# A new table of step numbers for the same steps in an attention and FFN kernel

## Chip, core and metric

The kernel runs on one core of one Trainium2 chip. The time is that of the device, in microseconds, of that core; three runs are given by their median. The profile is one execution, taken by the hardware's profiler.

## What is computed

```python
def phi(x):
    proj = np.einsum('bhsd,df->bhsf', x, w_phi)
    proj = proj - np.max(np.abs(proj), axis=-1, keepdims=True)
    return np.concatenate([np.exp(proj), np.exp(-proj)], axis=-1)
q_p, k_p = (phi(q), phi(k))
kv = np.einsum('bhsf,bhsd->bhfd', k_p, v)
z = np.sum(k_p, axis=2)
num = np.einsum('bhsf,bhfd->bhsd', q_p, kv)
den = np.einsum('bhsf,bhf->bhs', q_p, z)[..., None] + 1e-06
attn = num / den                       # 8 batches, 8 heads, 576 rows, 64 wide
x = attn.transpose(0, 2, 1, 3).reshape(4608, 512)
h = x @ w_in                           # 512 -> 2048
out = (h * np.cos(h)) @ w_out          # 2048 -> 512
```

All of it is float32.

## The kernel before

The work is cut into 3678 steps. A step is a short run of instructions on one engine: TensorE (PE), VectorE (DVE), ScalarE (ACT), GpSimd (POOL), or SyncE (SP), which issues the DMAs. The program builds the steps from loops, each with the steps that it depends on and the buffers that it takes and uses; then the list ORDER gives the sequence in which they are recorded, by their numbers. Each engine works off its own steps in that sequence. So ORDER sets what stands behind what in the five queues, and with that also when a buffer comes free.

There are three kinds of work.

Attention goes in 32 units of two heads (u0 to u31). In a unit, q_mm and q_end (L550, L553) project q on PE into three PSUM banks; q_copy (L561, L563) copies them out on ACT; DVE (L567, L575, L576), POOL (L581), DVE (L585) and POOL (L589) find and subtract the maximum; exp_q (L660) is four activations on ACT. k_mm and k_end (L596, L621) project k; k_max and k_neg (L634, L637) on DVE; exp_k (L654) on ACT reads the projection in its PSUM bank, eight activations to a half. kv_mm (L700, L706) is the first product on PE, kv_out (L712) its copy on ACT, and x_mm (L735, L741) the second product, from kv and exp_q. DVE divides, transposes, and SP stores the result to DRAM (L772, L776).

The weights w_in and w_out are converted in 16 pieces: SP loads raw words, ACT scales them (L410, L411), DVE works on their bits, ACT and DVE split them in a high and a low part (wi, wo), SP stores these to DRAM and loads them again later, since only three pieces of each kind have room (r.load, L511).

The FFN goes over nine chunks of 512 tokens. Chunks wait for the attention's results of their tokens, which SP loads (L820, L823, L1097; the tokens over 512 of each batch are gathered, L1102, in eight small DMAs to a tile). The first product is plain for three chunks (L955) and in seven half-size products of 256 columns for others (L907), or of 512 columns for the last two (L1182); ACT and DVE take the cosine (L962, L963, L981, L985, L988) and split the result (gh, gl); the second product is mm2 (L1004 to L1006, L1294 to L1296). Every float32r product is three matmuls, high by high, high by low and low by high.

PSUM has eight banks of 512 columns. A step that needs a bank gets the one whose last user stands earliest in ORDER:

```python
for x in (steps[i] for i in ORDER):
    for b in x.take:
        if b.ring == "bank":
            b.slot = min(range(len(banks)), key=lambda i: last(owner[i]))
```

So with another ORDER the same step writes another bank, and waits for another reader. The other buffers are rings of fixed size (x_raw 4, gh 3, eq 3 and so on). Exponentials and cosines need different tables on ACT; where one follows the other, a table load (ACT_TABLE_LOAD) stands between.

Of the kernel before, what the change touches and what calls it, by code (L numbers as in the profile page):

```python
# [25 lines left out]
def phi_attention_then_cos_ffn(ctx: ExitStack, tc: tile.TileContext, qkT, vS, w_phi, w_in, w_out, out):  # L26
# [41 lines left out]
    class Step:  # L68
# [19 lines left out]
        0, 42, 1, 3, 1265, 2, 4, 5, 7, 44, 6, 8, 9, 59, 46, 17, 64, 10, 65, 11, 18, 19, 58, 68, 83, 23, 47, 24,  # L88
        43, 12, 27, 45, 20, 48, 124, 1266, 21, 16, 60, 22, 13, 62, 61, 14, 50, 25, 1267, 63, 26, 15, 49, 86, 30,
        28, 1268, 31, 66, 1269, 99, 1270, 67, 32, 51, 71, 1271, 84, 33, 29, 1284, 72, 103, 52, 1272, 73, 53, 85,  # L90
        140, 1273, 87, 88, 104, 57, 101, 89, 1280, 1281, 142, 100, 56, 102, 125, 108, 90, 165, 55, 141, 91, 143,
        107, 54, 144, 35, 74, 105, 69, 146, 1274, 1275, 34, 147, 1276, 106, 112, 92, 109, 1277, 70, 93, 36, 113,
        37, 38, 1278, 114, 94, 126, 150, 148, 181, 1279, 128, 127, 145, 39, 95, 129, 130, 185, 98, 182, 40, 75,
        149, 183, 97, 131, 76, 1285, 96, 132, 206, 166, 187, 153, 188, 133, 77, 134, 154, 111, 78, 1286, 115,
        168, 1287, 184, 110, 186, 79, 191, 1295, 1288, 167, 135, 222, 169, 247, 41, 170, 1289, 116, 171, 189,
        155, 137, 224, 117, 226, 156, 138, 190, 172, 136, 223, 80, 227, 1290, 139, 118, 81, 225, 151, 173, 209,
        174, 194, 152, 119, 175, 228, 207, 229, 1291, 195, 232, 230, 196, 120, 208, 1292, 248, 231, 263, 1506,
        210, 176, 288, 212, 157, 211, 1296, 213, 179, 158, 121, 178, 265, 235, 122, 177, 1511, 159, 160, 180,
        264, 192, 214, 236, 82, 1512, 237, 197, 269, 193, 215, 266, 289, 267, 216, 123, 161, 238, 1505, 268,
        271, 270, 217, 1507, 249, 272, 1297, 304, 251, 162, 219, 252, 250, 218, 306, 305, 163, 198, 253, 273,  # L100
        307, 221, 254, 1509, 199, 255, 220, 1513, 329, 233, 308, 276, 310, 311, 256, 234, 277, 1510, 200, 257,
        278, 314, 309, 1514, 1508, 312, 290, 201, 330, 1298, 240, 1299, 292, 1314, 239, 1300, 1515, 345, 293,
        1516, 279, 313, 1301, 291, 1517, 368, 347, 258, 1302, 294, 317, 348, 1303, 1518, 318, 353, 259, 202,
        349, 319, 260, 1528, 1304, 296, 261, 274, 350, 203, 262, 320, 354, 241, 204, 346, 1305, 385, 1537, 1519,
        242, 275, 1306, 164, 351, 1307, 352, 1529, 295, 384, 297, 355, 243, 298, 1538, 390, 332, 386, 331, 1530,
        1308, 244, 281, 1539, 245, 280, 387, 1309, 1531, 333, 299, 407, 335, 334, 358, 205, 1293, 1540, 336,
        303, 1520, 388, 1315, 300, 282, 283, 302, 1546, 1564, 337, 1312, 301, 246, 284, 369, 1521, 1310, 338,
        316, 285, 339, 1316, 315, 1541, 1317, 392, 1318, 370, 1319, 1522, 371, 372, 321, 389, 446, 391, 1523,
        373, 1563, 374, 322, 340, 287, 393, 286, 375, 424, 344, 1524, 323, 1547, 341, 1325, 376, 343, 324, 1320,
        423, 429, 325, 342, 394, 326, 357, 397, 377, 327, 1321, 1569, 356, 425, 378, 427, 359, 409, 1532, 1542,  # L110
        1567, 428, 1322, 398, 1525, 411, 410, 412, 1543, 1526, 1566, 1533, 430, 1565, 1548, 413, 361, 447, 432,
        1534, 1283, 1570, 485, 360, 1294, 379, 1527, 362, 383, 1535, 363, 1549, 415, 380, 1573, 1536, 1550,
        1326, 414, 382, 364, 1544, 381, 1574, 1551, 463, 1571, 1545, 1552, 468, 1572, 1553, 469, 1568, 433, 395,
        416, 426, 1554, 365, 417, 396, 1327, 1575, 1328, 1559, 472, 1560, 1329, 431, 1282, 1330, 448, 1331,
        1576, 462, 1561, 450, 502, 451, 466, 1562, 449, 1586, 408, 1577, 328, 467, 418, 366, 1578, 452, 1555,
        421, 454, 1332, 1344, 400, 1557, 524, 419, 367, 1587, 464, 420, 399, 1311, 453, 422, 436, 507, 1333,
        1621, 434, 1324, 1588, 435, 1334, 488, 1595, 1335, 465, 401, 471, 455, 508, 1336, 402, 456, 1337, 511,
        403, 487, 437, 457, 1596, 501, 489, 1579, 438, 470, 404, 459, 439, 505, 458, 405, 503, 460, 490, 475,
        440, 1338, 461, 441, 563, 442, 1323, 473, 504, 1339, 491, 527, 474, 486, 1604, 506, 493, 406, 443, 1580,
        1622, 492, 476, 444, 509, 1597, 494, 478, 1581, 1558, 495, 510, 477, 496, 540, 1605, 498, 526, 542, 500,  # L120
        479, 514, 1623, 480, 499, 1342, 481, 1598, 497, 482, 1589, 1599, 483, 528, 1582, 1590, 1627, 1606, 1583,
        515, 1591, 543, 541, 1556, 1584, 530, 1607, 1592, 1585, 1625, 546, 1608, 1593, 1600, 544, 1609, 545,
        1601, 529, 1594, 1624, 1345, 1626, 445, 532, 525, 1602, 564, 531, 1610, 1629, 1603, 1346, 1631, 547,
# [1317 lines left out]
```

## Time and profile before

| | |
|---|---|
| median of 3 runs | 1037.19 us (1036.08 to 1038.19) |
| span of the profiled execution | 1034.7 us |
| mean granted TensorE clock | 0.998 |
| PE busy | 1024.1 us, 99% |
| weight loads (PEld) | 865.8 us, 84% |
| DVE, ACT, POOL busy | 742.0, 786.6, 147.6 us |
| first matmul starts, last ends | 1.12 us, 1031.0 us |

The times of the rows below are microseconds from the start of that execution. A timeline row gives the start, the time from the first start to the last end of the instructions that it merges, engine, line and operation, the tiles written and read (buffer numbers left out), shape and count; in brackets stands the idle time of the engine just before and what ended it. Float32 matmuls (L550 to L741) leave two records each, the others one. Matmuls are pipelined, and their ends are modelled.

### The profile page before, as it was taken

How to read it: one execution, taken by the hardware profiler on the slowest of the kernel's cores; microseconds unless marked ns; L12 is line 12 of the kernel's file. 1: busy time of each engine (PE TensorE's matmuls, PEld its weight loads, DVE VectorE, ACT ScalarE, POOL GpSimd, SP SyncE). 2: the span in 40 equal slices, each digit the busy share in tenths (PEclk: the TensorE clock that was granted, in tenths of full speed). 3: DMA queues.
4: the chain of work that ended last, by engine and by line, in shares of the span. 5: the costliest groups of instructions: out<-in, count | busy, mean ns of one | idle time of the engine just before them, and what ended most of it. 6: DMA issues, size and time to landing. Idle time of an engine off the chain costs nothing.

```text
span 1034.7 us, 23513 instructions
## 1 busy us (share of the span) xinstructions
PE 1024.1 (99%) x9402; PEld 865.8 (84%) x9402; DVE 742.0 (72%) x1418; ACT 786.6 (76%) x1602; POOL 147.6 (14%) x231
## 2 busy tenths in 40 slices
PE   9998999999999999999999999999999999999998
PEld 6786788888878888988889898888889988888886
DVE  7999998999888877765677457686565566655542
ACT  6999999898778778787789958887678465655432
POOL 4342242201101001201112011132001000000000
PEclk9999999999999999999999999999999999999999
DMA  7666587247667644678336762567427823453134
GB/s 252 192 213 207 177 257 248 89 159 256 222 232 273 209 137 158 224 262 304 116 112 218 254 234 69 176 239 257 162 77 249 293 74 92 166 210 153 41 133 153
DMA packets 86893, 195.22 MB, mean 189 GB/s; under 512 B 20608, under 2 KB 41216, under 8 KB 82944
## 3 DMA queue, kind: packets, MB, share of 16 engines
q1 hardware_dynamic: 86640, 193.66, 55.4%
q8 instruction: 74, 1.21, 0.5%
q14 instruction: 35, 0.29, 0.1%
q10 hardware_dynamic: 144, 0.07, 0.0%
HBM read 145.46 MB, written 48.23 MB: 187 GB/s over the span
## 4 chain that ended last, share of the span: by engine, by line
PE 89%; DVE 4%; ACT 3%; DMA 2%; issue 1%; SPq 0%; ACTq 0%; DVEq 0%
PE bank L907 15%; PE bank L955 10%; PE bank L1004 9%; PE bank L1005 9%; PE bank L1006 9%; PE bank L1182 8%; PE bank L700 6%; PE bank L735 5%; PE bank L1295 3%; PE bank L1294 3%; PE bank L1296 3%; PE bank L550 3%; PE bank L596 3%; PE bank L706 1%; PE bank L642 1%; PE bank L553 1%
## 5 line engine op out<-in xcount | busy, mean ns | idle before, releaser
L1004 PE MATMUL bank<-wo,gh 128*128 128x512 f32 x448 | 179.3, 400 | 0.0
L1005 PE MATMUL bank<-wo,gh 128*128 128x512 f32 x448 | 175.1, 391 | 0.0
L1006 PE MATMUL bank<-wo,gl 128*128 128x512 f32 x448 | 174.9, 390 | 0.0
L589 POOL TENSOR_TENSOR pq<-pq,bq 128x288 f32<-128x288 f32 x128 | 114.0, 922 | 174.2 <-DVE bq L585 123.5
L654 ACT ACTIVATE ek<-bank,mk 128x128 f32<-128x128 f32 x464 | 128.2, 418 | 4.6 <-DVE mk L637 4.4
L54 DVE TENSOR_TENSOR gl<-g,gh 128x512 fp32r<-128x512 f32 x128 | 89.4, 702 | 31.7 <-ACT gh L49 31.2
L49 ACT ACTIVATE gh<-g 128x512 fp32r<-128x512 f32 x128 | 81.3, 641 | 28.4 <-DVE g L988 13.3
L1004 PEld LDWEIGHTS bank<-wo,gh 128*128 128x128 f32 x448 | 84.3, 188 | 19.4 <-issue 2.2
L981 DVE SCALAR_TENSOR_TENSOR g<-g,hs 128x512 f32<-128x512 int32 x112 | 76.5, 689 | 33.1 <-ACT g L977 30.5
L1006 PEld LDWEIGHTS bank<-wo,gl 128*128 128x128 f32 x448 | 84.1, 188 | 18.5
L581 POOL COPY m<-m 32x36 f32<-32x36 f32 x96 | 32.9, 342 | 456.2 <-DVE m L576 400.2
L1005 PEld LDWEIGHTS bank<-wo,gh 128*128 128x128 f32 x448 | 84.4, 188 | 14.6
L985 ACT ACTIVATE g<-g,halfpi 128x512 f32<-128x512 f32 x112 | 79.0, 720 | 19.6 <-DVE g L981 19.1
L988 DVE TENSOR_TENSOR g<-hs,g 128x512 f32<-128x512 f32 x112 | 75.8, 687 | 21.5 <-ACT g L985 21.2
L660 ACT ACTIVATE eq<-pq 128x576 f32<-128x576 f32 x128 | 81.2, 713 | 4.0 <-PE bank L735 2.5
L907 PE MATMUL bank<-xh_t,wi 128*128 128x256 f32 x512 | 83.2, 285 | 0.3 <-ACT pq L561 0.3
L907 PEld LDWEIGHTS bank<-xh_t,wi 128*128 128x128 f32 x512 | 72.8, 190 | 4.8 <-issue 0.7
L919 ACT ACTIVATE hs<-bank 128x256 f32<-128x256 f32 x128 | 47.4, 393 | 36.2 <-PE bank L907 30.0
L735 PEld LDWEIGHTS bank<-kv,eq 128*64 128x64 f32 x2048 | 65.6, 140 | 10.4 <-issue 3.7
L735 PE MATMUL bank<-kv,eq 128*64 128x65 f32 x2048 | 70.9, 226 | 2.8 <-ACT ek L654 2.8
L700 PE MATMUL bank<-vs,ek 128*64 128x65 f32 x2048 | 66.4, 223 | 0.5 <-ACT pq L561 0.5
L700 PEld LDWEIGHTS bank<-vs,ek 128*64 128x64 f32 x2048 | 62.6, 138 | 4.4 <-ACT hs L963 0.8
(140 smaller groups left out, 2230.2 us busy)
## 6 DMA issues: line engine op xcount, KB each, us to landing
wi<-wi_parts SPq DMA_DIRECT2D x25, 1792.0 KB, 8.5
wo<-wo_parts SPq DMA_DIRECT2D x30, 1024.0 KB, 5.7
qk<-qkT SPq DMA_DIRECT2D x31, 640.0 KB, 5.4
x_raw<-xs SPq DMA_DIRECT2D x47, 256.0 KB, 4.3
vs<-vS SPq DMA_DIRECT2D x32, 325.0 KB, 4.7
wi_raw<-w_in SPq DMA_DIRECT2D x8, 1024.0 KB, 6.7
wo_raw<-w_out SPq DMA_DIRECT2D x8, 1024.0 KB, 6.6
xs<-xt SPq DMA_DIRECT2D x128, 64.0 KB, 3.1
```

The source lines that it names most:

```text
L49: ACT.activation(out=out, in_=in_, func=AF.Copy, scale=1.0)
L54: eng.tensor_tensor(out=out, in0=in_, in1=hi.bitcast(F32), op=ALU.subtract)
L589: qeng.tensor_tensor(out=d["pq"][:, c], in0=d["pq"][:, c], in1=d["bq"][:, c], op=ALU.subtract)
L654: ACT.activation(out=e[:, g, s * P:(s + 1) * P], in_=pk[:, g, :], func=AF.Exp, scale=1.0 - 2.0 * s, bias=d["lk" if s == 0 else "mk", i][:, ...
L700: PE.matmul(out=acc[c:c + 64, n, i, :], lhsT=e[:, s, P * n + c:P * n + c + 64], rhs=vs[b["v"].slot][:, 2 * s + i, :], start=(s == 0 and i ...
L735: PE.matmul(out=ps[64 * h:64 * h + 64, 65 * g:65 * g + 65], lhsT=d["eq", j][:, n, c:c + 64], rhs=d["kv"][:, 2 * n + j, :], start=h not in ...
L907: PE.matmul(out=out, lhsT=w[:, part, block, j * P:(j + 1) * P], rhs=d[x, name][:, j * HC:(j + 1) * HC], start=start and k == 0, stop=k == ...
L955: PE.matmul(out=bank(b), lhsT=w[:, part, 2 * r + kt // 2, kt % 2 * P:(kt % 2 + 1) * P], rhs=d.get(("from", kt), d)[x, kt], start=(k == 0), ...
L1004: PE.matmul(out=a, lhsT=gh[:, t], rhs=w[:, 0, r], start=first, stop=False)
L1005: PE.matmul(out=a, lhsT=gh[:, t], rhs=w[:, 1, r], start=False, stop=False)
L1006: PE.matmul(out=a, lhsT=gl[:, t], rhs=w[:, 0, r], start=False, stop=last)
L1182: PE.matmul(out=bank(bank_b), lhsT=w[:, part, block, j * P:(j + 1) * P], rhs=d[x, name, j], start=start and k == 0, stop=k == 5, skip_grou ...
```

## The change

Only the numbers in ORDER are in another sequence. The steps, what they cost by the program's own account, their dependencies and buffers are the same. The table's rows tell a reader nothing, so the diff is cut to its first and last lines. (The new table has fewer lines, so in the listings of the program after, a line below it has a number that is smaller by 44: L735 is L691, L660 is L616.)

```diff
--- before.py
+++ after.py
@@ -85,211 +85,167 @@
     ORDER = [
-        0, 42, 1, 3, 1265, 2, 4, 5, 7, 44, 6, 8, 9, 59, 46, 17, 64, 10, 65, 11, 18, 19, 58, 68, 83, 23, 47, 24,
...
-        3595, 3661, 3662, 3665, 3666, 3669, 3667, 3670, 3668, 3673, 3671, 3672, 3675, 3674, 3676, 3677,
+        0, 3, 42, 4, 5, 1, 59, 64, 1265, 45, 6, 65, 44, 7, 17, 58, 68, 2, 8, 46, 9, 19, 18, 20, 47, 21, 62, 63, 1266, 10, 25, 22, 26, 11,
...
+        3674, 3677,
     ]
```

What it moves is shown at three places. In the names, bank_69 to bank_76 are the PSUM banks 0 to 7.

First, ACT where units 7 to 9 meet. Before, with L985 the cosine, L410 and L411 the scaling of a weight, L660 exp_q of unit 7, L654 exp_k of unit 9, L49 a split and L561 q_copy of unit 9:

```order
L985 ACTIVATE g<-g,halfpi 128x512 x2
L410 ACTIVATE wo_t_1496<-wo_raw 128x1024
L411 ACTIVATE wo_t_1498<-wo_raw 128x1024
L660 ACT_TABLE_LOAD
L660 ACTIVATE eq<-pq 128x576 x4
L654 ACTIVATE ek<-bank_70,mk 128x128 x8
L49 ACTIVATE gh<-g 128x512
L561 ACTIVATE pq<-bank_69 128x512
```

After, from q_copy of unit 8 on, with L616 exp_q of unit 7 in two pairs, L918 and L919 a chunk's copy, L668 kv_out, L941 the cosine:

```order
L519 ACTIVATE pq<-bank_72 128x2x64
L517 ACTIVATE pq<-bank_70 128x512
L616 ACTIVATE eq<-pq 128x576 x2
L918 ACTIVATE g<-bank_76 128x512
L919 ACTIVATE hs<-bank_76 128x512
L668 ACTIVATE kv<-bank_73 128x260
L616 ACTIVATE eq<-pq 128x576 x2
L941 ACT_TABLE_LOAD
L941 ACTIVATE g<-g,halfpi 128x512 x2
L668 ACTIVATE kv<-bank_70 128x260
L941 ACTIVATE g<-g,halfpi 128x512
```

The two pairs of exp_q now stand ahead of the cosines and of the table load, and exp_k of unit 9 behind them. On PE at the same place, before, with L550 and L553 the projection of q of unit 9 and L735 and L741 x_mm of unit 7:

```order
L550 MATMUL bank_69<-qk,wphi 128x512
L550 MATMUL bank_75<-qk,wphi 128x512
L553 MATMUL bank_73<-qk,wphi 128x128
L735 MATMUL bank_70<-kv,eq 64x65 x16
L735 MATMUL bank_69<-kv,eq 64x65 x16
L741 MATMUL bank_69<-kv,eq 64x65 x4
```

After, with L656 and L662 kv_mm of unit 8, L691 and L697 x_mm of unit 7, L506 the projection of q of unit 9:

```order
L656 MATMUL bank_70<-vs_88,ek 64x65 x32
L662 MATMUL bank_70<-vs_88,ek 64x130 x4
L691 MATMUL bank_76<-kv,eq 64x65 x16
L697 MATMUL bank_76<-kv,eq 64x65 x4
L506 MATMUL bank_73<-qk,wphi 128x512
L506 MATMUL bank_71<-qk,wphi 128x512
L691 MATMUL bank_75<-kv,eq 64x65 x16
```

x_mm of unit 7 stands directly behind kv_mm of unit 8, its two halves are apart, and it writes banks 7 and 6 instead of 1 and 0.

Second, PE at the projection of q of unit 16. Before, L553 is q_end, twelve matmuls behind its q_mm (L550, not in these rows), which wrote banks 0 and 5:

```order
L1006 MATMUL bank_70<-wo,gl 128x512
L1004 MATMUL bank_71<-wo,gh 128x512
L1005 MATMUL bank_71<-wo,gh 128x512
L1006 MATMUL bank_71<-wo,gl 128x512
L553 MATMUL bank_69<-qk,wphi 128x128
L1004 MATMUL bank_75<-wo,gh 128x512
```

After, L506 is q_mm and L509 q_end:

```order
L961 MATMUL bank_75<-wo,gh 128x512
L962 MATMUL bank_75<-wo,gl 128x512
L506 MATMUL bank_74<-qk,wphi 128x512
L506 MATMUL bank_69<-qk,wphi 128x512
L509 MATMUL bank_72<-qk,wphi 128x128
L960 MATMUL bank_70<-wo,gh 128x512
```

q_end now follows its q_mm and writes bank 3; before it wrote bank 0, as the first half of its q_mm had.

Third, SP's queue late in the attention. L511 reloads converted weights, L1102 is the gather of eight DMAs, L1064 stores a result. Before:

```order
L511 DMA wi<-wi_parts_97 128x2x1792
L1102 DMA x_raw<-xs_tail 32x8x32 x8
L511 DMA wi<-wi_parts_90 128x2x1792
L1064 DMA out<-o 128x512
L511 DMA wi<-wi_parts_91 128x2x1792
```

After, with L467 the reloads, L492 a load of v, L1053 and L1058 loads of x, L1020 a store:

```order
L467 DMA wi<-wi_parts_97 128x2x1792
L1053 DMA x_raw<-xs 128x512
L492 DMA vs_89<-vS 128x650
L467 DMA wi<-wi_parts_90 128x2x1792
L467 DMA wi<-wi_parts_91 128x2x1792
L1020 DMA out<-o 128x512
L467 DMA wi<-wi_parts_92 128x2x1792
L467 DMA wo<-wo_parts_105 128x2048
L1058 DMA x_raw<-xs_tail 32x8x32 x8
L467 DMA wi<-wi_parts_93 128x2x1792
```

The gather stood between the first and the second reload and now stands behind the fifth.

## Rows read from the trace of the kernel before

**Rows 1.** The page: busy time of each engine with its share of the span and its instructions; and, from the costliest groups, the weight loads of L1004 (busy us, mean ns of one).

```profile
PE 1024.1 (99%) x9402; PEld 865.8 (84%) x9402; DVE 742.0 (72%) x1418; ACT 786.6 (76%) x1602; POOL 147.6 (14%) x231
...
L1004 PEld LDWEIGHTS bank<-wo,gh 128*128 128x128 f32 x448 | 84.3, 188 | 19.4 <-issue 2.2
```

**Rows 2.** PE's timeline at seven places, matmuls alone.

```profile
85.84 1.10 PE L735 MATMUL bank<-kv,eq 128*64 128x65 f32 x32
87.46 2.09 PE L700 MATMUL bank<-vs,ek 128*64 128x65 f32 x64 [0.52 <-ACT pq L561]
...
93.92 0.49 PE L553 MATMUL bank<-qk,wphi 128*128 128x128 f32 x2
97.19 3.56 PE L735 MATMUL bank<-kv,eq 128*64 128x65 f32 x64 [2.78 <-ACT ek L654]
100.59 0.40 PE L741 MATMUL bank<-kv,eq 128*64 128x65 f32 x8
...
107.21 0.40 PE L1006 MATMUL bank<-wo,gl 128*128 128x512 f32 x1
107.78 0.49 PE L553 MATMUL bank<-qk,wphi 128*128 128x128 f32 x2 [0.17 <-ACT kv L712]
...
125.55 0.49 PE L621 MATMUL bank<-wphi,qk 128*128 128x128 f32 x2
126.16 0.49 PE L553 MATMUL bank<-qk,wphi 128*128 128x128 f32 x2
126.40 0.71 PE L955 MATMUL bank<-xh_t,wi 128*128 128x512 f32 x2
...
299.40 0.39 PE L1005 MATMUL bank<-wo,gh 128*128 128x512 f32 x1
299.63 0.39 PE L1006 MATMUL bank<-wo,gl 128*128 128x512 f32 x1
301.12 0.49 PE L553 MATMUL bank<-qk,wphi 128*128 128x128 f32 x2 [1.11 <-ACT pq L561]
...
766.27 0.49 PE L553 MATMUL bank<-qk,wphi 128*128 128x128 f32 x2
767.02 0.74 PE L907 MATMUL bank<-xh_t,wi 128*128 128x256 f32 x4 [0.26 <-ACT pq L561]
```

**Rows 3.** Busy time by stretch: from and to, its length, busy us of PE, PEld, DVE, ACT and POOL with counts, then the granted TensorE clock, the DMA share and GB/s.

```profile
75.00:150.00 75.00, 71.40 (x1001) 57.74 (x999) 70.92 (x161) 74.82 (x178) 25.13 (x42) 0.98 0.65 206
...
97.20:100.60 3.40, 3.40 (x66) 3.40 (x68) 3.30 (x7) 3.40 (x12) 0.00 (x0) 0.53 1.05 399
...
298.00:302.50 4.50, 3.39 (x16) 2.51 (x15) 4.12 (x6) 4.20 (x9) 0.00 (x0) 1.00 1.00 384
...
200.00:800.00 600.00, 598.10 (x5478) 517.79 (x5477) 434.12 (x827) 486.95 (x1007) 79.16 (x122) 1.00 0.58 198
```

**Rows 4.** PE's timeline from 778 to 795 us, matmuls alone.

```profile
778.34 0.40 PE L907 MATMUL bank<-xl_b,wi 128*128 128x256 f32 x2
778.67 2.09 PE L700 MATMUL bank<-vs,ek 128*64 128x65 f32 x64
...
781.03 2.03 PE L735 MATMUL bank<-kv,eq 128*64 128x65 f32 x64
782.90 0.40 PE L741 MATMUL bank<-kv,eq 128*64 128x65 f32 x8
783.23 0.74 PE L907 MATMUL bank<-xh_t,wi 128*128 128x256 f32 x4
783.81 0.40 PE L907 MATMUL bank<-xl_t,wi 128*128 128x256 f32 x2
784.05 0.64 PE L907 MATMUL bank<-xh_t,wi 128*128 128x256 f32 x4
784.53 0.40 PE L907 MATMUL bank<-xl_t,wi 128*128 128x256 f32 x2
785.37 0.71 PE L907 MATMUL bank<-xh_b,wi 128*128 128x256 f32 x4 [0.44 <-DVE g L981]
...
793.78 0.40 PE L907 MATMUL bank<-xl_b,wi 128*128 128x256 f32 x2
794.27 0.74 PE L907 MATMUL bank<-xh_b,wi 128*128 128x256 f32 x4
```

**Rows 5.** ACT's timeline from 87.9 to 95 us.

```profile
87.94 1.34 ACT L985 ACTIVATE g<-g,halfpi 128x512 f32<-128x512 f32 x2
89.17 1.17 ACT L410 ACTIVATE wo_t<-wo_raw 128x1024 f32<-128x1024 f32 x1
...
91.38 1.28 ACT L660 ACT_TABLE_LOAD   x1
92.68 2.40 ACT L660 ACTIVATE eq<-pq 128x576 f32<-128x576 f32 x4
```

**Rows 6.** SP's timeline from 777 to 786 us: the DMAs that it issued, and from the first issue to the last landing or next issue as the trace merges them.

```profile
777.21 0.53 SPq L511 DMA_DIRECT2D wi<-wi_parts  x1
777.80 7.76 SPq L1102 DMA_DIRECT2D x_raw<-xs_tail  x8
785.65 0.85 SPq L511 DMA_DIRECT2D wi<-wi_parts  x1
```

**Rows 7.** The page's DMA issues: reloads of wi, KB of each, median us from issue to landing.

```profile
wi<-wi_parts SPq DMA_DIRECT2D x25, 1792.0 KB, 8.5
```

362 rows, old and new, of the table ORDER are left out of this document.

## The prediction

> **What bounds the kernel now.** I read the busy shares first: TensorE (PE) is busy 1024.1 of 1034.7 us, the next engine 76% [rows 1]. The change touches nothing but the order of the steps, so the question is what PE loses between one step and the next. A busy share can't answer that. One 512-column matmul is drawn 0.39 us long, but the next one starts 0.23 us later (299.40 to 299.63, [rows 2]): the bars overlap, so a pause of up to 0.16 us vanishes and every longer one is drawn that much too short. I therefore read PE's timeline by starts, and take as lost what lies between two starts beyond the usual spacing of that form. The Trainium skill, Perfetto Trace Analysis (Identifying the Most-Contended Engine), says that matmul busy time misjudges the room left and that the busy share of weight loads is to be used; that share is 84% [rows 1]. By it the room would be 16% of the span, an estimate of some 169 us. The rows speak against taking it as room for an order: a weight load of 0.188 us [rows 1] sits inside each 0.23 us spacing, and no order changes that spacing.
>
> Next I read who was waited for. From 200 to 800 us PE is busy 598.1 of 600 [rows 3]; it starts one matmul right behind the other. The losses sit in few places, and at each the matmul waited for a PSUM bank that ACT (or, once, DVE) had still to read, or for a reloaded weight tile. More than half of the loss lies between 85 and 130 us; from 75 to 150 us ACT is busy 74.82 of 75 us [rows 3]: there ACT, with attention, weight conversion and the first chunks all at once, paces the kernel.
>
> **What the order before loses.** Each term is start to start, less the usual spacing.
> 1. 87.46: 32 records of L735 from 85.84; 64 take 1.87 us (781.03 to 782.90, [rows 4]), so 32 take 0.94; 1.62 passed: 0.68 lost [rows 2].
> 2. 97.19: a pair of L553 takes 0.24 (126.16 to 126.40) and a change of array shape adds 0.09 (term B below); 3.27 passed: 2.94 lost [rows 2].
> 3. The clock. Over 97.20 to 100.60 the granted clock reads 0.53, that is 1.2 GHz nearly throughout, right after that idle stretch [rows 3]. The 64 records of L735 took 3.40 instead of 1.87: 1.53 lost [rows 2, 4]. The pause at 301.12, 1.11 us of idle, cost no clock: it reads 1.00 from 298 to 302.5 [rows 2, 3].
> 4. 107.78: 0.57 against 0.23: 0.34. 126.16: 0.61 against 0.24: 0.37. 301.12: 1.49 against 0.23: 1.26. 767.02: 0.75 against 0.24: 0.51 [rows 2].
> 5. 785.37: 0.84 against the 0.24 of two 256-column matmuls (783.81 to 784.05): 0.60. 794.27: 0.49 against 0.24: 0.25 [rows 4].
> The sum is 0.68 + 2.94 + 1.53 + 0.34 + 0.37 + 1.26 + 0.51 + 0.60 + 0.25 = 8.48 us.
>
> **What the new order does at these places.** Nothing is added or removed: the matmuls, activations, DVE and GpSimd instructions and DMAs are the same in number.
>
> At 97.19 the matmuls are x_mm of unit 7. They write the bank that exp_k of unit 9 reads, and on ACT that read stood last in a row: two cosines 1.23 (start to start), the two scalings of a weight 2.21, a table load 1.30, four exp_q, drawn 2.40, and the first eight exp_k, after which PE started: 9.25 us from 87.94 [rows 5]. PE's own work meanwhile ended by 94.25 (93.92 + 0.33, [rows 2]). The difference is term 2. Now (the first place shown) x_mm of unit 7 stands behind kv_mm of unit 8, it writes banks 7 and 6, which a chunk's copy and an earlier unit's DVE product left, and its inputs, the exp_q pairs, come ahead of the cosines and of the table load. Counted from q_mm of unit 8, ACT has up to the second exp_q pair the scalings 2.21, four exp_q 2.40 and six copies, none longer than a cosine of 0.61, so at most 3.7: 8.3 us. PE has in that time 12 matmuls of 512 columns 2.76, q_end 0.24, x_mm of unit 6 with 72 records 2.10, kv_mm, drawn 2.09 without its tail of eight (87.46, [rows 2]), and a k_mm: 7.2 and the k_mm, by its 16 small matmuls near 1. It fits, with up to 1 us to spare where the copies are shorter. Without the long pause the slow clock goes too.
>
> At 301.12 the single matmul q_end wrote the bank that its own q_mm had filled, so it had to wait until ACT had copied that one. Now q_end follows q_mm at once and into another bank; nothing of q_copy is waited for (the second place).
>
> At 785.37 and 794.27 the wait was for wi: its reload was issued at 777.21 and takes 8.5 us to land, which is 785.7; the next was issued at 785.65, and 8.5 later is 794.2 [rows 6, 7]. Between the two stood a gather of eight DMAs that held SP's queue from 777.80 for 7.76 us. SP's queue is in order, so everything behind it was late. Now five reloads stand ahead of the gather (the third place). One reload stands directly behind it still, and may be late by what 794.27 was, 0.25.
>
> At 87.46, 107.78, 126.16 and 767.02 the bank that was waited for is another in the new order, or the step that reads it stands earlier. These I take as gone, too.
>
> **B. Shape changes on PE.** Going from weights of 128 columns to ones of 64 and back costs: 778.34 to 778.67 is 0.33 instead of 0.24 (+0.09), 782.90 to 783.23 is 0.33 where 8 records of L741 take about 0.23 (+0.10), and the first four after it take 0.58 instead of 0.48 (+0.10) [rows 4]: 0.29 a round trip. Counted in the two orders, the shape changes 154 times before and 148 after: three round trips, 0.87 us. Switching between 256 and 512 columns, of which there are more now, shows no cost in the rows: I take nothing.
>
> **C. Table loads on ACT** rise from 70 to 76, each 1.28 us [rows 5]: 7.7 us of ACT. By place in the order, both have 7 of them where PE stands at 50 to 150 us, and all extra ones come after that, where ACT has room: from 200 to 800 us it is busy 487 of 600 [rows 3]. I take nothing; without that cover it would be up to 7.7.
>
> **D. New waits.** No row shows them. From below: nothing; from above: as much as the order before has, 8.5, for the same steps on the same engines. The nearest rows are the small losses, those under 0.7 us: 0.68 + 0.34 + 0.37 + 0.51 + 0.60 + 0.25 = 2.75, where the order left just too little. I take 2.0, somewhat less, since the place I followed leaves up to 1 us of room, and keep 0 and 8.5 for the range.
>
> **Sum** against the profiled execution: 1034.7 - 8.5 - 0.9 + 2.0 = 1027.3. The median of three runs, 1037.19, is 2.5 above that span; that stays: 1029.8 us.
>
> **Rivals.**
> R1, the waits stay where ACT is full. Between 75 and 150 us ACT has no slack, and the same ACT work has to be done before PE can go on. Then terms 1 to 3 and two of 4 (0.68 + 2.94 + 1.53 + 0.34 + 0.37 = 5.86) come back in other places, and only 1.26 + 0.51 + 0.85 and 0.87 are won, 3.5: 1033.7. For it: ACT's 74.82 of 75 [rows 3]. Against: at the longest wait ACT was not short of time but of order, with cosines and a table load ahead of what PE waited for, and PE has other matmuls to run meanwhile.
>
> R2, slower. A long pause costs 2.94 and then 1.53 for the clock, 4.47 together. If ACT falls so far behind in that same stretch that three such pauses arise, 13.4 us, the 9.4 won are more than spent: 1037.2 - 9.4 + 13.4 = 1041.2. Two, 8.9, would not do it. For it: up to 1 us of room at the place I followed is less than one exp_k of 2 us that slips ahead. Against: three are needed, and the one in the trace had a table load and 2.2 us of weight scaling in the queue ahead of it.
>
> R3, the pauses only move: as many new ones as old, 8.5, and the shape changes alone are won: 1036.3. For it: PE busy 99%. Against: each of the old ones has a cause in the order that I could follow, and the new order has it no longer.
>
> **How the numbers follow.** Forecast 0.70, R1 0.17, R3 0.07, R2 0.06. No new waits would give 1027.8, and runs scatter by about 1, so the low end is 1026.5. Towards the top the range takes in most of R1 with up to 1.3 more: 1035.0. That leaves out R2, R3 and the edges, 2 in 10. A difference under 0.2%, 2.1 us, can't be told from none: faster means under 1035.1, which is the forecast and most of R1, 0.82; within is R3 and the rest of R1, 0.11; slower 0.07.
>
> **What would show it.** Right: in the profile after, x_mm of unit 7 starts without idle behind ACT's exp_k, the granted clock stays 1.00 from 75 to 125 us, q_end of unit 16 follows its q_mm, the reloads of wi around 780 us land before their matmuls, and what PE loses by starts is about 2 us in pieces under 0.7. Wrong: a new pause over 2 us with a slow stretch behind it, or ACT waited for in the same 75 to 150 us (R1), or PE waiting on loads of qk, of which some are now issued closer to their use.

## The result and the profile after

The kernel after takes 1044.58 us (median of 6 runs, 1043.25 to 1045.75), the kernel before 1037.09 in the same session (6 runs, 1035.88 to 1040.17): a ratio of 1.0066, 95% interval 1.0052 to 1.0081. It is slower by 0.66%, where 1029.8 and faster was forecast. The span of the profiled execution is 1041.6 us, against 1034.7.

The page of the kernel after begins with the busy times; the part with the costliest groups gives, for each, busy time and mean ns of one:

```profile
PE 1026.9 (99%) x9402; PEld 865.6 (83%) x9402; DVE 764.1 (73%) x1418; ACT 797.0 (77%) x1608; POOL 164.7 (16%) x231
...
L545 POOL TENSOR_TENSOR pq<-pq,bq 128x288 f32<-128x288 f32 x128 | 132.5, 1063 | 219.3 <-DVE bq L541 147.9
...
L937 DVE SCALAR_TENSOR_TENSOR g<-g,hs 128x512 f32<-128x512 int32 x112 | 80.4, 721 | 36.5 <-ACT g L933 31.5
L54 DVE TENSOR_TENSOR gl<-g,gh 128x512 fp32r<-128x512 f32 x128 | 92.4, 728 | 19.8 <-ACT gh L49 19.4
...
L944 DVE TENSOR_TENSOR g<-hs,g 128x512 f32<-128x512 f32 x112 | 83.1, 750 | 24.6 <-ACT g L941 24.5
```

Against [rows 1], ACT's 10.4 us more are mostly the table loads of term C. But VectorE (DVE) and GpSimd (POOL) have as many instructions as before and are busy 22.1 and 17.1 us longer: the same instructions took longer. Before, the four groups had a mean of 922, 689, 702 and 687 ns, in the order of the rows above.

The windows answer to [rows 3]; the third window is new (columns: window, its length, then busy us of PE, PEld, DVE, ACT, POOL, the granted clock, DMA share, GB/s):

```profile
75.00:150.00 75.00, 72.33 (x970) 59.02 (x966) 70.95 (x155) 72.25 (x168) 24.94 (x35) 0.98 0.59 180
97.20:100.60 3.40, 3.40 (x25) 2.65 (x25) 3.37 (x8) 3.40 (x12) 3.40 (x4) 1.00 0.00 0
103.35:107.37 4.02, 4.02 (x74) 3.84 (x73) 3.96 (x6) 3.97 (x9) 0.00 (x0) 0.58 1.01 335
200.00:800.00 600.00, 595.65 (x5452) 513.20 (x5451) 450.56 (x825) 487.18 (x994) 86.45 (x119) 1.00 0.58 196
```

The slow clock of 97 us is gone, but there is another one at 103 to 107, and from 200 to 800 us PE now misses 4.35 us instead of 1.9. PE's timeline, read by starts as in [rows 2], shows where:

```profile
83.70 0.49 PE L509 MATMUL bank<-qk,wphi 128*128 128x128 f32 x2 [0.80 <-ACT hs L919]
...
93.28 1.10 PE L691 MATMUL bank<-kv,eq 128*64 128x65 f32 x32
...
100.92 0.49 PE L509 MATMUL bank<-qk,wphi 128*128 128x128 f32 x2
102.93 0.49 PE L509 MATMUL bank<-qk,wphi 128*128 128x128 f32 x2 [1.52 <-ACT ek L610]
...
158.96 0.40 PE L961 MATMUL bank<-wo,gh 128*128 128x512 f32 x1
160.34 0.50 PE L962 MATMUL bank<-wo,gl 128*128 128x512 f32 x1 [0.99 <-DVE gl L54]
...
305.45 0.49 PE L509 MATMUL bank<-qk,wphi 128*128 128x128 f32 x2
305.70 0.48 PE L960 MATMUL bank<-wo,gh 128*128 128x512 f32 x1
...
306.25 0.40 PE L962 MATMUL bank<-wo,gl 128*128 128x512 f32 x1
308.20 0.96 PE L911 MATMUL bank<-xh_b,wi 128*128 128x512 f32 x3 [1.55 <-DVE o L1000]
...
571.61 0.49 PE L552 MATMUL bank<-wphi,qk 64*128 64x128 f32 x4
573.69 0.94 PE L552 MATMUL bank<-wphi,qk 64*128 64x128 f32 x12 [1.59 <-issue]
...
785.54 0.40 PE L863 MATMUL bank<-xl_t,wi 128*128 128x256 f32 x2
785.87 1.16 PE L552 MATMUL bank<-wphi,qk 64*128 64x128 f32 x16
```

The old pauses are gone as forecast. x_mm of unit 7 (93.28) starts without idle, q_end of unit 16 (305.45) passes in 0.25, no product waits for wi around 785. The new ones: 102.93 is 2.01 after 100.92 where a pair takes 0.24, 1.77 lost, and the slow clock behind it stretches kv_mm to 4.02 where 2.41 is usual (789.11 to 791.52): 1.61. 160.34 lost 1.38 - 0.23 = 1.15, 308.20 1.95 - 0.23 = 1.72, 573.69 1.8 (four of sixteen records take 0.27), 83.70 1.1. Taken over all of PE's steps (start to next start, less the median of that kind of step in the two traces), the losses over 0.15 us sum to 9.2 us in 13 pieces before and 16.9 us in 26 pieces after. With a median of its own for each kind of next step they are 9.5 in 13 and 15.2 in 23, so such a sum holds to some 2 us. All losses, by stage:

| us | before | after | after_thin | after_fill |
|---|---|---|---|---|
| 0 to 50 | 1.1 | 2.6 | 0.8 | 0.6 |
| 50 to 100 | 4.7 | 3.0 | 3.0 | 4.9 |
| 100 to 200 | 2.4 | 7.1 | 1.3 | 2.7 |
| 200 to 500 | 2.7 | 4.1 | 1.5 | 1.4 |
| 500 to 600 | 0.9 | 4.4 | 2.7 | 2.4 |
| 600 to 800 | 3.2 | 1.5 | 1.4 | 1.4 |
| whole span | 15.5 | 23.8 | 11.7 | 14.4 |

(The last two columns are experiments below.) How one of the new pauses comes about stands in the rows of DVE and, last, of POOL ahead of 308.20:

```profile
297.72 2.51 DVE L54 TENSOR_TENSOR gl<-g,gh 128x512 fp32r<-128x512 f32 x2
300.16 1.30 DVE L944 TENSOR_TENSOR g<-hs,g 128x512 f32<-128x512 f32 x1
301.38 1.83 DVE L375 SCALAR_TENSOR_TENSOR wi_t<-wi_raw,wi_t 128x1024 uint32<-128x1024 uint32 x1
303.24 0.69 DVE L378 TENSOR_SCALAR wi_t<-wi_t 128x1024 uint32<-128x1024 uint32 x1
303.97 1.23 DVE L397 TENSOR_TENSOR wi_t<-wi_t,wi_t 128x1024 f32<-128x1024 f32 x1
305.11 0.69 DVE L54 TENSOR_TENSOR xl_t<-x_raw,xh_t 128x512 fp32r<-128x512 f32 x1
305.72 1.22 DVE L411 TENSOR_TENSOR wi_t<-wi_t,wi_t 128x1024 f32<-128x1024 f32 x1
306.85 0.69 DVE L54 TENSOR_TENSOR xl_b<-x_raw,xh_b 128x512 fp32r<-128x512 f32 x1
307.45 0.69 DVE L1000 TENSOR_TENSOR o<-bank,o 128x512 f32<-128x512 f32 x1
...
297.32 4.80 POOL L545 TENSOR_TENSOR pq<-pq,bq 128x288 f32<-128x288 f32 x4 [30.60 <-DVE mk L593]
```

While POOL's four subtractions run (297.32 to 302.12), a DVE instruction of 512 columns takes 1.29 to 1.30 instead of 0.69, and one of 1024 takes 1.83 instead of 1.24. Three of them come after 298.9: 0.6 each, 1.8 in all. DVE has no gap over 0.04 from there to L1000 at 307.45, which reads the bank that PE waits for. PE lost 1.72: it is the stretching, carried along in DVE's queue.

It happens to instructions that read both operands from SBUF. Of those on L54, L937 and L944 (461 in all), 57 run beside a subtraction on POOL for over a fifth of their time, and 26 did before. Instructions that read a PSUM bank aren't touched (L716: 281 ns alone, 277 beside POOL). POOL's own subtraction takes 0.81 alone, 1.2 here (4.80 for four) and at most 1.83. The Trainium skill, SBUF — State Buffer (SBUF: two separate sides), says that the two engines have one pair of SBUF ports in common, that a VectorE operation with two SBUF inputs and a GpSimd operation that reads SBUF exclude each other, and that the second waits for the whole instruction of the first. The trace agrees here: beside each other the two take turns, one pair in 1.22 us (300.16 to 301.38). But the wait isn't always one instruction long: in after_fill, an experiment below, a subtraction waited 4.32 us behind five VectorE instructions.

### The profile page after: what moved, and what is told of

Read it like the earlier page. It is cut to its first block, busy times and chain, and to the rows that moved or that the text cites. A ratio compares the mean times of both kernels' runs of the same rounds, so it can differ in the third digit from the quotient of the medians.

```text
span 1041.6 us, 23491 instructions
## 1 busy us (share of the span) xinstructions
PE 1026.9 (99%) x9402; PEld 865.6 (83%) x9402; DVE 764.1 (73%) x1418; ACT 797.0 (77%) x1608; POOL 164.7 (16%) x231
## 4 chain that ended last, share of the span: by engine, by line
PE 73%; DVE 14%; ACT 8%; issue 3%; DMA 1%; POOL 1%; SPq 0%; DVEq 0%; ACTq 0%; POOLq 0%
PE bank L863 15%; PE bank L960 8%; PE bank L961 8%; PE bank L1138 8%; PE bank L962 7%; PE bank L911 6%; PE bank L691 4%; PE bank L656 4%; PE bank L1252 3%; PE bank L1251 3%; PE bank L1250 3%; ACT ek L610 2%; PE bank L506 2%; PE bank L552 1%; DVE mk L590 1%
## 5 line engine op out<-in xcount | busy, mean ns | idle before, releaser
L545 POOL TENSOR_TENSOR pq<-pq,bq 128x288 f32<-128x288 f32 x128 | 132.5, 1063 | 219.3 <-DVE bq L541 147.9
L937 DVE SCALAR_TENSOR_TENSOR g<-g,hs 128x512 f32<-128x512 int32 x112 | 80.4, 721 | 36.5 <-ACT g L933 31.5
L54 DVE TENSOR_TENSOR gl<-g,gh 128x512 fp32r<-128x512 f32 x128 | 92.4, 728 | 19.8 <-ACT gh L49 19.4
L944 DVE TENSOR_TENSOR g<-hs,g 128x512 f32<-128x512 f32 x112 | 83.1, 750 | 24.6 <-ACT g L941 24.5
L49 ACT ACTIVATE gh<-g 128x512 fp32r<-128x512 f32 x128 | 81.6, 644 | 25.1 <-DVE g L944 12.9
L941 ACT ACTIVATE g<-g,halfpi 128x512 f32<-128x512 f32 x112 | 79.5, 720 | 27.0 <-DVE g L937 26.4
L616 ACT ACTIVATE eq<-pq 128x576 f32<-128x576 f32 x128 | 80.8, 711 | 7.4 <-POOL pq L545 5.1
L691 PEld LDWEIGHTS bank<-kv,eq 128*64 128x64 f32 x2048 | 64.6, 138 | 7.8 <-issue 3.3
L691 PE MATMUL bank<-kv,eq 128*64 128x65 f32 x2048 | 70.1, 223 | 0.0
L656 PEld LDWEIGHTS bank<-vs,ek 128*64 128x64 f32 x2048 | 63.9, 141 | 6.0 <-issue 2.2
L656 PE MATMUL bank<-vs,ek 128*64 128x65 f32 x2048 | 67.7, 226 | 0.0
```

What stands on the lines that cost most here:

```text
L49: ACT.activation(out=out, in_=in_, func=AF.Copy, scale=1.0)
L54: eng.tensor_tensor(out=out, in0=in_, in1=hi.bitcast(F32), op=ALU.subtract)
L545: qeng.tensor_tensor(out=d["pq"][:, c], in0=d["pq"][:, c], in1=d["bq"][:, c], op=ALU.subtract)
L656: PE.matmul(out=acc[c:c + 64, n, i, :], lhsT=e[:, s, P * n + c:P * n + c + 64], rhs=vs[b["v"].slot][:, 2 * s + i, :], start=(s == 0 and i ...
L691: PE.matmul(out=ps[64 * h:64 * h + 64, 65 * g:65 * g + 65], lhsT=d["eq", j][:, n, c:c + 64], rhs=d["kv"][:, 2 * n + j, :], start=h not in ...
L944: DVE.tensor_tensor(out=n["g"], in0=m["hs", r], in1=n["g"], op=ALU.mult)
```

## The experiments

The theories. **POOL**: the new order lets GpSimd's subtraction meet these VectorE instructions, and the stretching makes the new waits. **MARGIN**: the order leaves no room anywhere, and anything late makes them. **TABLE**: the six more table loads do.

**The subtraction cut short.** Both kernels, 16 of 288 columns.

```diff
-            c = slice(j * HALF, (j + 1) * HALF)
+            c = slice(j * HALF, j * HALF + 16)
             qeng.tensor_tensor(out=d["pq"][:, c], in0=d["pq"][:, c], in1=d["bq"][:, c], op=ALU.subtract)
```

> The kernel before, with GpSimd's subtraction of the maximum (four instructions of 288 columns a unit) cut to 16 columns; the other columns are left as they are, so the output is another. It is the partner of after_thin. Theory POOL: GpSimd's subtraction stretches those VectorE instructions that read both operands from SBUF while it runs (0.69 us alone, up to 1.30 beside it in the trace after); the order before has few such meetings (26 of 461), so here little is won: 1034 to 1037 us, VectorE busy 735 to 740 us instead of 742. Theory MARGIN (the new order leaves no room anywhere, and ordinary scatter on any engine makes the new waits): the same 1034 to 1037.

> The kernel after with the same cut of GpSimd's subtraction to 16 of 288 columns (the rest is left out, so the output is another). Theory POOL: with the stretching gone VectorE's busy time falls from 764 to 735 to 740 us, and of the 7.5 us by which the kernel after is slower at least 5.5 go: from 3 below to 2 above before_thin, that is 1031 to 1039. Theory MARGIN: GpSimd is not special, 4 to 8 us above before_thin, 1039 to 1044. Theory TABLE (the six extra table loads, 7.7 us of ACT): the same 1039 to 1044.

Measured: before_thin 1037.59 us, ratio to before 0.9999 (0.9987 to 1.0012); after_thin 1031.31, ratio 0.9935 (0.9918 to 0.9951). The sign turns: without long subtractions the new order is 0.64% faster than the old one. The same stretch of DVE in after_thin, and POOL's row:

```profile
289.58 1.33 DVE L54 TENSOR_TENSOR gl<-g,gh 128x512 fp32r<-128x512 f32 x2
290.84 0.70 DVE L944 TENSOR_TENSOR g<-hs,g 128x512 f32<-128x512 f32 x1
291.46 1.24 DVE L375 SCALAR_TENSOR_TENSOR wi_t<-wi_raw,wi_t 128x1024 uint32<-128x1024 uint32 x1
...
289.17 2.44 POOL L545 TENSOR_TENSOR pq<-pq,bq 128x16 f32<-128x16 f32 x4 [30.60 <-DVE mk L593]
```

All three are back at their usual time, and the pause of 308 is gone. So are those of 160 and 528. MARGIN and TABLE alone would have left the new order behind.

**No table loads.** The exponential in place of the cosine.

```diff
-                ACT.activation(out=n["g"], in_=n["g"], func=AF.Sin, bias=halfpi, scale=1.0)
+                ACT.activation(out=n["g"], in_=n["g"], func=AF.Exp, bias=halfpi, scale=1.0)
```

> The kernel before with the exponential in place of the cosine in the FFN, so that ACT never loads another table (the output is another); partner of after_notab. It gives ACT 70 x 1.28 = 90 us back. All theories: the wait at 97 us shrinks by at least the table load in ACT's row there; 1030 to 1035 us.

> The kernel after with the exponential in place of the cosine, so no table is loaded (the output is another). Theory TABLE: the six extra loads were what made it slower, so without any it is within 2 us of before_notab or below it. Theory POOL: VectorE's row stays stretched (busy near 764 us), the waits for its products stay, and it stays 4 us or more above before_notab, less only what ACT's waits gave. Theory MARGIN: waits for ACT go, those for VectorE stay: 2 to 6 us above before_notab.

Measured: before_notab 1036.02 us, ratio 0.9982 (0.9972 to 0.9992); after_notab 1039.16, ratio 1.0010 (1.0000 to 1.0020). before_notab lies 1 us above its range, which all theories had. The difference of the two is in MARGIN's range and below POOL's 4 us. The new order is still 3.1 us behind, with the pauses of 160 and 308 where they were and DVE busy 763.8 us. TABLE falls as the cause, since after_thin keeps all loads and is faster; that ACT with some 90 us less to do hides a part (4.4 of 7.5 us) shows how little ACT has to spare.

**The subtraction on VectorE.** No work left out, no long instruction on GpSimd.

```diff
-    Q_DVE = range(0)
+    Q_DVE = range(13, 32)
```

> The kernel after, with the subtraction of the maximum on VectorE instead of GpSimd for units 13 to 31, at the same places of the order; all work is done. It adds some 4 x 0.36 us x 19 = 27 us to VectorE (by columns from 0.60 us for 512) where it is 86% busy at most, and takes GpSimd's long instructions out of everything behind about 160 us. Theory POOL: what the kernel after loses behind 150 us beyond after_thin goes (1.9 at 161, 0.6 at 200 to 250, 1.8 at 308, 1.8 at 528 to 531, about 6 us): 1037 to 1040 us. Theory MARGIN: VectorE's 27 us more in an order without room make new waits: 1043 to 1050 us.

> The kernel after with the subtraction on VectorE in all 32 units; all work is done. Theory POOL: up to 160 us VectorE is busy 24.1 to 24.6 of 25 us, part of it the stretching itself (some 10 us), and gets some 19 us more of its own: the later part is won as in after_dve_late, the earlier one is level or worse by up to 8: 1035 to 1047 us. Theory MARGIN: worse than after_dve_late by more than 8 us.

> The kernel before with the subtraction on VectorE for units 13 to 31, the partner of after_dve_late; all work is done. Theory POOL: the order before has hardly a meeting of GpSimd with a VectorE instruction of two SBUF operands behind 160 us, so nothing is won: 1035 to 1038 us. Theory MARGIN: some new waits, 1037 to 1042 us.

(after_dve_all has range(32) there.) Measured: after_dve_late 1046.76 us, ratio 1.0085 (1.0063 to 1.0107); after_dve_all 1058.12, ratio 1.0193 (1.0167 to 1.0220); before_dve_late 1038.28, ratio 1.0006 (0.9994 to 1.0019). All three are in MARGIN's ranges and outside POOL's (before_dve_late by 0.3 us, less than its runs scatter): the pauses of 308 and 528 went, but others came at 675 to 689 and 712 (2.0, 1.1, 0.8, 0.5 us). The 76 subtractions (0.45 us each, 34 us of DVE) cost the order before nothing that can be told, and the new order as much as the stretching. So MARGIN holds for DVE in the new order: the subtractions made it late, and PE paid.

**The late terms alone.** The order before up to 745 us, then that of after, and q_end of unit 16 (644) one product back; the diff shows only the last.

```diff
-        644, 1885, 1453, 1853, 647,
+        1885, 1453, 1853, 644, 647,
```

> The order of before up to its position 2850 (about 745 us), behind it the order of after, and q_end of unit 16 one product further back (behind 1853 instead of ahead of it); all work is done. It asks whether the late terms of the prediction hold (1.26 at 301, 0.51 at 767, 0.85 at 785 to 794: 2.6 us in all, less 0.3 that after loses there) where the order before is kept for the rest: 1034 to 1035.5 us by the prediction's terms and by theory POOL, since no unit's subtraction is left behind 770 us; 1037 or more if the terms were no losses, or come back elsewhere.

Measured: 1036.22 us, ratio 0.9983 (0.9970 to 0.9995), 1.15 less than before. The pauses at 301, 767, 785 and 794 are gone; here q_end of unit 16:

```profile
302.73 0.39 PE L965 MATMUL bank<-wo,gl 128*128 128x512 f32 x1
302.96 0.38 PE L512 MATMUL bank<-qk,wphi 128*128 128x128 f32 x2
303.10 0.48 PE L963 MATMUL bank<-wo,gh 128*128 128x512 f32 x1
```

From 300 to 350 us the loss is 0.3 instead of 1.5, from 750 to 800 0.4 instead of 1.9: 2.7 us, as the terms say. In the profiled run 1.6 us were lost anew at 59.0 and 0.9 at 482.6, where the order is that of before. At 59.0 the trace leads back to a load: ACT's split of x waited 2.33 us for x_raw (to 56.35), DVE's split behind it 1.66, and PE 1.41 for the k_max behind that. At 482.6 PE waited for no semaphore, 0.70 us. The median of 1036.22 lies between the two ranges that were expected, so the run shows that these pauses go, and not that the whole time falls by as much. It is the one version with all the work that is faster than both kernels.

**Mending the waits one by one.** What PE waits for is put ahead of other work on DVE (dvefix, the first diff; dots stand for numbers left out); a product is put between kv_mm and the k_mm that idled without a semaphore (code, the second diff); both and three more moves (repaired).

```diff
-        1606, 1599, ..., 1592,
+        1606, ..., 1592, 1599, 1600,
...
-        2391, ..., 2366,
+        ..., 2366, 2391,
...
-        1450, ..., 1930, 1451, ..., 1864,
+        ..., 1930, ..., 1864, 1450, 1451,
```

```diff
-        943, ..., 969, ..., 2524,
+        943, ..., 2524, 969,
```

> The order after with four VectorE steps (and one ACT step) further back, all work done: at 161 us times 1599 (and its split 1600) stands behind the split 1592 that PE waits for; at 528 reduce 2391 behind the split 2366; at 308 the weight steps 1450 and 1451 behind the output copy 1864. GpSimd's subtraction and the stretching stay. Theory POOL (each wait there is a chain of VectorE instructions that GpSimd stretches by 1.4 to 2.2 us; putting what PE waits for ahead of others of 1.2 us takes it away): the waits of 1.37, 0.72 and 1.81 go, 3.9 us, 1040 to 1041.5 us. Theory MARGIN (what is put back is late in its turn): 1043 to 1046 us.

> The order after with k_mm of unit 24 (969) one product further back, behind 2524, so that a product of 0.8 us stands between kv_mm of unit 23 and it; all work is done. Theory CODE: the 1.86 us at 574, in which PE waited for no semaphore, are a wait for its own instructions (a fetch of 16 KB ends 1.28 us before the wait does, in three runs of this order at the same instruction): with the slower product between, the fetch has time, 1042.5 to 1043.5 us. If it is something else (the load of qk, a bank): 1044 to 1045 us and the idle time stays at k_mm.

> The order after with the steps moved as in dvefix and in code, and three more: the ACT step 1308 behind the chunk's copy 1518 (83.7 us, 1.12 lost there), the split 1522 behind exp_k 392 (102.9, 0.5 of 1.76), times 201 ahead of k_max 306 (69.4, 0.4 of 0.53); all work is done. If each wait is local and can be mended by itself: 3.9 + 1.8 + 1.1 + 0.5 + 0.4 = 7.7 us, and 1.5 more where the slow clock behind 102.9 goes: 1035.3 to 1037.5 us. Theory MARGIN: half of it or more comes back elsewhere, 1040 us or more.

Measured: dvefix 1045.18 us, ratio 1.0076 (1.0062 to 1.0090); code 1043.76, 1.0062 (1.0049 to 1.0075); repaired 1044.66, 1.0076 (1.0062 to 1.0089). dvefix and repaired miss, as MARGIN expected: the pauses went and came back a few us later, in dvefix 160 at 167 (1.4), 308 at 316 (0.6), 528 at 532 (2.3) and 535 (1.3). The one at 532 can be followed, on PE and then on ACT in dvefix:

```profile
529.50 0.40 PE L867 MATMUL bank<-xl_b,wi 128*128 128x256 f32 x2
532.10 0.54 PE L581 MATMUL bank<-wphi,qk 128*128 128x128 f32 x2 [2.19 <-ACT ek L614]
...
527.33 0.73 ACT L945 ACTIVATE g<-g,halfpi 128x512 f32<-128x512 f32 x1 [1.22 <-DVE g L941]
...
528.58 1.28 ACT L614 ACT_TABLE_LOAD   x1
529.87 2.17 ACT L614 ACTIVATE ek<-bank,mk 128x128 f32<-128x128 f32 x8
```

The reduce that was put back on DVE held up a cosine, behind it in ACT's queue stood a table load and exp_k, and PE waited for the bank that exp_k reads. The time that DVE lost came out here. The median of code lies between the ranges with and without theory CODE, and can't be told from that of after. In it the idle time of 573.69 shrank from 1.59 to 1.28 only and fell on the product that now stands there, so it isn't k_mm, its load or its bank that PE waited for:

```profile
571.62 0.74 PE L867 MATMUL bank<-xh_t,wi 128*128 128x256 f32 x4
573.65 0.40 PE L867 MATMUL bank<-xl_t,wi 128*128 128x256 f32 x2 [1.28 <-issue]
```

**A splice.** The order before to 58 us, repaired from there to 99 us, before (with mix's change) to 745, then after.

```python
# each part without the steps that stand in a part ahead of it
before[:268] + repaired[:431] + mix[:2850] + after
```

> The order before up to 58 us, the order of repaired from there to 99 us, the order before again (with q_end of unit 16 one product further back, as in mix) up to 745 us, then the order after; all work is done. From the losses of each by stage: before loses 4.7 us from 50 to 100 where repaired should lose 1.5, and 2.2 from 100 to 150 of which 1.3 follow the wait at 97; with mix's 2.9 that makes some 7 us less than before: 1030 to 1033 us. If the splice makes new waits at its ends, or ACT's full stretch gives back what is won: 1034 to 1037 us.

Measured: 1040.82 us, ratio 1.0039 (1.0026 to 1.0052). The splice at 99 us made its own waits: PE idled 2.61 at 103.96 for a split on ACT that a move of repaired had put behind exp_k, and 1.25 at 105.98. Splicing blind at the place where ACT is full doesn't pay.

**Which half of GpSimd's part.** after_thin also made GpSimd's step shorter, so that exp_q could start sooner. These keep its length.

```diff
-            c = slice(j * HALF, (j + 1) * HALF)
-            qeng.tensor_tensor(out=d["pq"][:, c], in0=d["pq"][:, c], in1=d["bq"][:, c], op=ALU.subtract)
+            for k in range(4):
+                c = slice(j * HALF + 16 * k, j * HALF + 16 * k + 16)
+                qeng.tensor_tensor(out=d["pq"][:, c], in0=d["pq"][:, c], in1=d["bq"][:, c], op=ALU.subtract)
```

```diff
+            c = slice(j * HALF, j * HALF + 16)
             qeng.tensor_tensor(out=d["pq"][:, c], in0=d["pq"][:, c], in1=d["bq"][:, c], op=ALU.subtract)
+            qeng.memset(d["bq"][:, j * HALF:(j + 1) * HALF], 0.0)
+            qeng.memset(d["bq"][:, j * HALF:j * HALF + 64], 0.0)
```

> The kernel before with each of GpSimd's subtractions of 288 columns done as four of 16 columns (64 of the 288 columns are subtracted, the rest is left as it is, so the output is another); partner of after_short4. GpSimd's step takes 0.9 to 1.6 us, as long as it was (0.8 to 1.25) or longer. Both theories: level with before, 1035 to 1039 us.

> The kernel after with each subtraction as four of 16 columns (the rest of the columns is left as it is, so the output is another). Theory STRETCH (VectorE's longer instructions are what costs): VectorE busy stays at 736 to 742 us, since an instruction of 16 columns holds it up by little, and the time is within 3 us of after_thin, 1031 to 1034.5 us. Theory LATENCY (exp_q comes too late because GpSimd takes long): GpSimd's time is back, so the loss is, too: 1040 us or more.

> The kernel after with each subtraction cut to 16 columns and two fills by GpSimd of 288 and 64 columns behind it (the rest of the columns is left as it is, so the output is another): about 0.8 us as before. Whether a fill stretches VectorE no row here shows. If VectorE's instructions beside it stay at 0.69, theory STRETCH gives 1031 to 1035 us and theory LATENCY 1040 or more; if they take 1.2 or more, both give 1040 to 1045 and the run tells nothing between them.

Measured: before_short4 1037.65 us, ratio 1.0002 (0.9991 to 1.0014); after_short4 1038.51, ratio 1.0005 (0.9995 to 1.0014); after_fill 1035.20, ratio 0.9973 (0.9961 to 0.9985). The groups of DVE and of POOL in after_fill:

```profile
L54 DVE TENSOR_TENSOR gl<-g,gh 128x512 fp32r<-128x512 f32 x128 | 86.8, 684 | 25.1 <-ACT gh L49 24.4
...
L946 DVE TENSOR_TENSOR g<-hs,g 128x512 f32<-128x512 f32 x112 | 75.9, 685 | 24.8 <-ACT g L943 24.6
...
L545 POOL TENSOR_TENSOR pq<-pq,bq 128x16 f32<-128x16 f32 x128 | 51.9, 406 | 218.0 <-DVE bq L541 148.7
...
L546 POOL MEMSET bq<- 128x288 f32 x128 | 45.9, 359 | 7.6
...
L547 POOL MEMSET bq<- 128x64 f32 x128 | 20.0, 156 | 7.4
```

GpSimd's step is 0.41 + 0.36 + 0.16 = 0.92 us, more than the 0.81 of an undisturbed subtraction, and nothing on DVE is stretched. Then the new order is faster than before by 0.27%. From after (1.0066) to after_fill (0.9973) lie 0.93%, some 9.6 us: the stretching, with GpSimd's step 0.14 shorter than its 1.06 in after. after_fill lies 0.2 us above STRETCH's range, and after_short4 between the ranges of both theories.

From after_fill to after_thin (0.37 us a step) lie another 0.38%, 3.9 us. Little of that is GpSimd's own length, for one place of after_fill alone loses as much (the two profiled runs differ by 2.7). Its rows, of POOL, DVE, ACT and PE:

```profile
67.97 4.32 POOL L545 TENSOR_TENSOR pq<-pq,bq 128x16 f32<-128x16 f32 x1
...
68.08 0.66 DVE L54 TENSOR_TENSOR xl_b<-x_raw,xh_b 128x512 fp32r<-128x512 f32 x1
68.67 1.20 DVE L397 TENSOR_TENSOR wi_t<-wi_t,wi_t 128x1024 f32<-128x1024 f32 x1
69.80 1.27 DVE L54 TENSOR_TENSOR xl_b<-x_raw,xh_b 128x512 fp32r<-128x512 f32 x2
71.00 1.21 DVE L411 TENSOR_TENSOR wi_t<-wi_t,wi_t 128x1024 f32<-128x1024 f32 x1
...
73.11 2.40 ACT L618 ACTIVATE eq<-pq 128x576 f32<-128x576 f32 x4 [2.86 <-POOL pq L545]
...
76.25 0.80 PE L913 MATMUL bank<-xh_t,wi 128*128 128x512 f32 x1 [1.96 <-ACT xh_t L49]
```

A subtraction of 16 columns, 0.22 us as the median, took 4.32: it stood until DVE had gone through five instructions with two SBUF operands, one behind the other without a gap (68.08 to 72.21). exp_q waited 2.86 us for GpSimd, the split xh_t stood behind exp_q on ACT, and PE idled 1.96 us and then ran at a granted clock of 0.55 (76.2 to 80.0): 12 matmuls took 6.65 us from start to start instead of 2.7. In after_thin the four subtractions were through before those five began. after_short4 has the same wait (4.22 us at 71.87), and its 512 subtractions have a mean of 322 ns against a median of 214, so a third of its step of 4 x 0.32 = 1.29 us is waiting too. So the two engines hold each other up in both directions. LATENCY is right that a late exp_q costs time, but what made it late here was mostly the wait for DVE; what GpSimd's plain length costs, the 0.14 us included, no run shows by itself. The time of the order before can't be told from its own in any of the runs with a cut subtraction.

## Why the prediction was wrong, point by point

**What bounds the kernel**: right. PE by starts, not by busy share, found every pause, before and after.

**Terms 1 to 5, 8.48 us**: right. All these pauses are gone in the profile after, with the slow clock of term 3, and mix, which takes those of 301, 767, 785 and 794 away alone, is faster by 1.15.

**B**, 0.87: not shown, and counted too widely. The 154 and 148 changes include those to and from weights of 64 rows (q_mm and k_mm). Of the kind that [rows 4] price, from 128 columns to 64 and back, the order before has 94 and the order after 96; what the other kind costs no run shows. The losses by steps differ by 8.3 us, the spans by 6.9, and what the 1.4 between them are stays open.

**C**, the table loads at nothing: no run takes just six away. They don't set the sign, since after_thin and after_fill keep them; but ACT has less room than "487 of 600" suggested, as notab and dvefix show.

**D, new waits, 2.0: this is the step that failed.** Of the 16.9 us in pieces over 0.15, at most 0.7 can be old ones (9.2 less the 8.48 that went), so D is about 16, or 14 by the other sum (15.2, less 9.5 - 8.48). Not only the value was wrong, but the bound of 8.5: "as much as the order before has, for the same steps on the same engines" took the durations to belong to the steps. They belong to the steps and to what runs beside them. The order decides what meets what: on three lines alone VectorE met GpSimd 31 times more, and DVE was 22.1 us longer busy with the same work. In a queue without gaps, DVE's from 298.9 to 308.1, all of it reached PE. Two things could have told: the mean of 922 ns of GpSimd's subtraction in the trace before, where one alone takes 808, and the code, where the steps of the two engines that get in each other's way carry a flag, port=True.

How much of D this is, the experiments bound: 9.6 us go with the stretching (after_fill), 13.6 (1.31%) with the waits in both directions and the length of GpSimd's step (after_thin). With that cause removed the rest of the sum nearly holds: without any new waits it gives 1027.8, after_thin measured 1031.3, and two long pauses left in it (1.73 at 99, 1.79 at 562) are together of the size of the 3.5 between them. That they fit so closely is luck, since B is in the 1027.8 and smaller losses are left out. The pause at 99 is a wait for exp_k on ACT that the order makes with or without GpSimd's long subtractions.

**The rivals.** R2 had the sign and part of the mechanism: 83.70, 102.93 and the slow clock behind it cost 4.5 us in the stretch where ACT is full. But most of the loss is elsewhere, and its cause was DVE beside GpSimd, which no rival had. R1 and R3 took new losses to be no more than old ones, as D did. The 0.07 for slower was too little, because every case was built on the durations of one trace. Of the prediction's signs of being wrong two came close to the letter: a pause with a slow stretch behind it (1.77 at 102.93, not over 2), and ACT waited for between 75 and 150 us (83.70 and 102.93).

What stays open: the 1.8 us at 573.69, in which PE waited for no semaphore. The profile of every run of the order after, or with only dvefix's, code's or repaired's moves, has it (1.0 to 1.7 us of idle) at the 5827th record of a matmul, whichever step stands there; before, mix and spliced don't have it at that record. In all the runs that have it a fetch of 16 KB on a queue for instructions ended 1.26 to 1.52 us before PE went on; in before, mix and spliced it ended 2.0 to 2.3 us ahead of the same record. The pause of mix at 482.6 has such a fetch 1.53 us before its end. That PE had run out of instructions fits, but no run shows it.

## What to carry to other kernels

A duration taken from one trace holds for what ran beside it there: before an order is judged, or searched, by such numbers, list which instructions of VectorE with two SBUF operands will run beside GpSimd, and give them the stretched time; a GpSimd instruction that comes up behind a row of them may have to wait for the whole row. In this order, fitted without room, lateness of a side engine became idle time of the bottleneck, and moving single steps sent much of that lateness on to the next wait. What an order is worth if the durations held can be measured: shorten the instruction that disturbs, in both versions, and compare.

## What the runs showed of the hardware

- Beside GpSimd's subtraction a VectorE instruction of 128x512 with both operands in SBUF takes up to 1.30 us instead of 0.69; instructions with a PSUM operand keep their time; a fill on GpSimd (359 ns for 128x288) disturbs none of them.
- The other way round, a GpSimd subtraction of 128x16, 0.22 us as the median, took 4.32 us beside five such VectorE instructions that followed each other without a gap (after_fill, 67.97), and 4.22 us in after_short4. So the two do not always take turns as they did at 300 us in after.
- Even k_neg, 128x4 with one SBUF operand, takes up to 776 ns beside it, where 156 is the median:

```profile
L593 DVE TENSOR_SCALAR mk<-mk x82: 104/156/776, 6.5 to 807.2; 128x4 f32<-128x4 f32 x50, 128x1 f32<-128x1 f32 x32
```

- An idle time of 1.52 us at 102.93 was followed by 4 us at a granted clock of 0.58, that is mostly 1.2 GHz, while idle times of 1.55 at 308.20 and 1.59 at 573.69 were not (1.00 from 308.2 to 312 and from 573.69 to 578). Two experiments differ in this at the same matmul: behind 1.96 us of idle after_fill ran at 0.55 (76.2 to 80.0), behind 2.04 us after_short4 at 1.00 (80.3 to 84.0).
